# A fused attention and two mixture layers on one core: a gather issued earlier on POOL, two groups of transposes put ahead of a product, and the last row tile finished in two halves

## The chip, the cores and the metric

The kernel runs on one core of one Trainium2 chip. The metric is the device time of one execution in microseconds (us). The kernel before took 614.89 us, the median of 3 runs (614.12 to 617.11). An engine name stands for an instruction queue that runs in order: PE (TensorE, matrix products and transposes), ACT (ScalarE), DVE (VectorE), POOL (GpSimd, which also issues the indirect DMAs) and SP (SyncE, which issues the weight loads).

## The reference

Three stages follow each other, cut here to what is computed:

```
attn = softmax(q k^T / 8, masked) v          # B=2, H=8, S=576, D=64: 4 heads local, 4 heads strided
x    = attn as [1152 tokens, 512]
# first layer: one expert of 8 for each token
e    = argmax(x @ w_gate + modality_bias[modality_id])
x1   = gate * (relu(x @ w1[e]) @ w2[e])      # w1 512x1024, w2 1024x512 for each expert
# second layer: all 4 experts for each token, weighted
out  = sum over e of p[:, e] * (relu(x1 @ w1b[e]) @ w2b[e])
```

## The kernel before

**Order.** All instructions are issued in the order in which the Python code calls them; there is no planner. Work of different stages is interleaved by hand, with small hooks that are called at fixed places of a loop. Each engine runs its own instructions in that order, and waits where a semaphore says so.

**Precision.** Every fp32 operand of a large product is split into a rounded high part (ACT, a cast) and the remainder (DVE, a subtraction), and each product is three matmuls (high by high, high by low, low by high). `split` (lines 979 to 982) is this pair; its rows carry L981 for ACT and L982 for DVE.

**First layer.** Tokens are sorted by expert into 11 tiles of 128 rows (0 to 10). `moe1` (line 1141) runs a loop over k = 0 to 11. Round k does the first product of tile k (`mm1`, four blocks of weights, L1161), between them the transposes of the hidden rows of tile k-1 (`htr`, i = 0 and 1, L1168, four transposes each, followed by a split into hh and hl), and then the second product of tile k-1 (`mm2`, u = 0 to 3, six matmuls each, L1182 to L1184). After each mm2 it calls `mid(tile, u)`, and at the end of the round `after(tile)`. The result y goes from ACT to the DRAM buffer `ye` (L1228, L1230). In round 11 there is no first product: the products of unit 0 of the second layer are called through `before_last(W, n)` instead, which is `second_layer_start` (line 1494). Its table says how many products are called at n = 0 to 4.

**Weights of the first layer.** A block of 512 KB is loaded by SP into one of 8 staging places (L177), split by ACT and DVE into one of a ring of 10 pairs, and used by PE. The split of a block stands in the code up to 10 blocks ahead of its use (`W.ahead`), and as soon as DVE has done its part the place is free, and the load of the block that is next for this place may go. With a new expert every block is really loaded; with the same expert as the tile before, the load is skipped.

**From the first layer to the second.** The second layer wants the tokens in another grouping, in 9 chunks of 128 rows (j = 0 to 8). `x2_gather(j)` (L1240) is an indirect DMA on POOL's queue that reads rows of `ye` by the index tile `cidx` into a tile `g`; five `g` tiles are used in turn, together with the gathers of the first layer (L987). Chunk 2 reads only rows that tiles 0 to 4 have written (`lim`, line 1239). `x2_prep(j)` prepares a chunk in two steps: four transposes on PE (L1272), a copy back on ACT (L1274), four sums on POOL (L1278 to L1281) and splits (L1285 on ACT, L1286 on POOL); the second step splits the four sums. The table `PREP` (line 1473) says behind which (tile, u) each step stands: chunk 0 at (4, 2) and (5, 0), chunk 1 at (5, 2) and (6, 0), chunk 2 at (6, 2) and (7, 0), chunk 3 at (8, 2) and (9, 0). On POOL the row gathers of the first layer (L711, L987, called by `xprep` in the first-product part of a round) stand in the same queue.

**Second layer.** 32 units (16 for the first four chunks, 16 for the last five); `m2_unit` (line 1393) makes seven products (L1405 to L1407) of each, in a Strassen-like form, with sums of weight blocks on POOL (L1345 to L1348) and splits of weights in pieces (`PC`, L1324 on ACT, L1325 on DVE). `m2_mm2` (line 1547) makes the second products of the units into five accumulators, one for each row tile i (L1554, L1555, L1557). The products of row tiles 3 and 4 of the last three units are kept back in the list `late` and run last; after the last product of a row tile DVE multiplies and adds (L1567), and POOL scatters the rows to the output (`scatter`, L1577 and L1578).

Of the kernel before, what the change touches and what calls it, by code (L numbers as in the profile page):

```python
# [25 lines left out]
DM = H * D  # L26
# [100 lines left out]
def fused_kernel(  # L127
# [581 lines left out]
    def with_rows(y, idx, n=NTOK):  # L709

        nc.gpsimd.indirect_dma_start(  # L711
            out=y[:, DM:], out_offset=None, in_=xx[:n, :], in_offset=bass.IndirectOffsetOnAxis(ap=idx, axis=0)
        )
# [265 lines left out]
    def split(dst_h, dst_l, src):  # L979

        nc.scalar.copy(dst_h, src)  # L981
        nc.vector.tensor_tensor(dst_l, src, dst_h.bitcast(F32), op=ALU.subtract)  # L982
# [15 lines left out]
    def x_parts(g, pt=None):  # L998
        pt = pt or x_transposed(g)
        xh = xp.tile([P, 512], F32R, name="xh")  # L1000
        xl = xp.tile([P, 512], F32R, name="xl")
        split(xh, xl, pt)
        return xh, xl
# [137 lines left out]
    def moe1(mp, tiles, W, gs, pool, mid, after, before_last):  # L1141
        n = len(tiles)
        xs, hs, ys = {}, {}, {}

        def xprep(k):
            g = gs.pop(k)
            y = mp.tile([P, XW], F32, name="y", bufs=3)
            with_rows(y, idx16[:, tiles[k] : tiles[k] + 1])
            xs[k] = x_parts(g) if k > 1 else x01[k]
            ys[k] = y  # L1150
            if k + 2 < n:
                gs[k + 2] = m1_gather(tiles[k + 2], pool)

        def mm1(k, ph, kc):
            xh, xl = xs[k]
            key = "1", tiles[k], kc
            wh, wl = W.out.pop(key)
            s = slice(P * kc, P * (kc + 1))
            for xx, ww, first, last in ((xh, wh, kc == 0, False), (xh, wl, False, False), (xl, wh, False, kc == KC - 1)):
                for i in range(2):  # L1160
                    nc.tensor.matmul(ph[i], xx[:, s], ww[:, 512 * i : 512 * (i + 1)], start=first, stop=last)  # L1161
            W.release(key)

        def htr(k, i, ht):
            pt = pst.tile([P, 512], F32, name="ps_a")
            for c in range(4):
                s = slice(512 * i + P * c, 512 * i + P * (c + 1))
                nc.tensor.transpose(pt[:, P * c : P * (c + 1)], hs[k][:, s], ident)  # L1168
            hh = mp.tile([P, 512], F32R, name="hh")
            hl = mp.tile([P, 512], F32R, name="hl")  # L1170
            split(hh, hl, pt)
            ht.append((hh, hl))

        def mm2(k, ht, py, u):
            key = "2", tiles[k], u
            wh, wl = W.out.pop(key)
            for i in range(2):
                kc = 2 * u + i
                hh, hl = ht[kc // 4]
                s = slice(P * (kc % 4), P * (kc % 4 + 1))  # L1180
                f = slice(512 * i, 512 * (i + 1))
                nc.tensor.matmul(py, hh[:, s], wh[:, f], start=(kc == 0), stop=False)  # L1182
                nc.tensor.matmul(py, hh[:, s], wl[:, f], start=False, stop=False)  # L1183
                nc.tensor.matmul(py, hl[:, s], wh[:, f], start=False, stop=(kc == FC - 1))  # L1184
            W.release(key)

        xprep(0)
        xprep(1)
        for k in range(n + 1):
            ht = []  # L1190
            most = min(k, 1)
            if k == n:
                before_last(W, 0)
            if k < n:
                ph = [psb.tile([P, 512], F32, name="ps_b") for _ in range(2)]
                mm1(k, ph, 0)
            if k > 0:
                htr(k - 1, 0, ht)
            W.ahead(RING, most)
            if k == n:  # L1200
                before_last(W, 1)
            if k < n:
                mm1(k, ph, 1)
            if k > 0:
                htr(k - 1, 1, ht)
            W.ahead(RING, most)
            if k < n:
                mm1(k, ph, 2)
                if 0 < k < n - 1:
                    xprep(k + 1)  # L1210
                W.ahead(RING, most)
                mm1(k, ph, 3)
                h = mp.tile([P, FF], F32, name="h")
                for i in range(2):
                    nc.scalar.activation(h[:, 512 * i : 512 * (i + 1)], ph[i], AF.Relu)
                hs[k] = h
                W.ahead(RING, 1 + most)
            if k > 0:
                py = psb.tile([P, 512], F32, name="ps_b")
                for u in range(4):  # L1220
                    mm2(k - 1, ht, py, u)
                    if k == n and u < 3:
                        before_last(W, 2 + u)
                    mid(tiles[k - 1], u)
                    if u < 3:
                        W.ahead(RING, 1)
                y = ys.pop(k - 1)
                nc.scalar.activation(y[:, :DM], py, AF.Copy, scale=y[:, DM : DM + 1])  # L1228
                t = tiles[k - 1]
                nc.scalar.dma_start(out=ye[(t + 1) * P : (t + 2) * P, :], in_=y)  # L1230
                W.ahead(RING, 1)
                after(t)
# [4 lines left out]
    def x2_gather(j):  # L1237
        g = gp.tile([P, XW], F32, name="g")
        lim = min(NSX + 1, j + E1 + 1, 2 * j + 2) * P
        nc.gpsimd.indirect_dma_start(  # L1240
            out=g, out_offset=None, in_=ye[:lim, :], in_offset=bass.IndirectOffsetOnAxis(ap=cidx[:, j : j + 1], axis=0)
        )
        gx[j] = g
# [13 lines left out]
    CHT = (4, 5)  # L1257
# [207 lines left out]
    first, prep = {}, {}  # L1465

    def first_layer_start(t):
        for j in {3: (0,), 4: (1,), 5: (2,), 7: (3,)}.get(t, ()):
            x2_gather(j)
        prep_step(t, 4)  # L1470

# [3 lines left out]
    def prep_step(t, u):  # L1475
        j = PREP.get((t, u))
        if j is not None:
            next(prep.setdefault(j, x2_prep(j)), None)
        if (t, u) in ((NST - 2, 1), (NST - 2, 3)):
            PC.put((u + 1) // 2)  # L1480

    def first_layer_mid(t, u):
        if t >= 1 and u in (1, 3):
            next(place, None)
        prep_step(t, u)

    def first_tmp(k):
# [6 lines left out]
    def second_layer_start(W, n):  # L1494

        if n == 0:
            m2_bank.extend(psb.tile([P, 512], F32, name="ps_b") for _ in range(3))
            first["u"] = m2_unit(0, first_tmp)
        if n == 2:
            PC.put(2)  # L1500
        for _ in range((2, 0, 2, 2, 1)[n]):
            next(first["u"])


# [4 lines left out]
    W = Weights(m1b + m2b, raws, len(m1b))  # L1509
# [33 lines left out]
    for q in range(2):  # L1543
        t = xh2.rearrange("p q c t -> p (q c t)"), xl2.rearrange("p q c t -> p (q c t)")
        HT.append([x[:, NH * q : NH * (q + 1)].rearrange("p (f t h o) -> p f t h o", f=2, h=2, o=HP) for x in t])

    def m2_mm2(u, i, fh, cols=slice(0, DM)):

        c, e, fb = units2[u]
        hh, hl = (h[:, fh, i].rearrange("p h o -> p (h o)") for h in h_of(u))  # L1550
        wh, wl = (w[:, 512 * fh : 512 * (fh + 1)][:, cols] for w in WT["w", u])
        po = m2_acc[i][:, cols]
        part = (c, e, i) == (1, E2 - 1, CHT[1] - 1)
        nc.tensor.matmul(po, hh, wh, start=(fb == 0 and fh == 1), stop=False, skip_group_check=part)  # L1554
        nc.tensor.matmul(po, hh, wl, start=False, stop=False, skip_group_check=part)  # L1555
        last = fb == FC // 2 - 1 and fh == 0
        nc.tensor.matmul(po, hl, wh, start=False, stop=last, skip_group_check=part)  # L1557
        if last:
            j = CH0[c] + i
            if e == 0:  # L1560
                rows[j] = raws[KC + i // 2][:, DM * (i % 2) : DM * (i % 2 + 1)]
            pe = ext2[:, j, 1 + e : 2 + e]
            row = rows[j][:, cols]
            if e == 0:
                nc.vector.tensor_scalar(row, po, pe, None, op0=ALU.mult)
            else:
                nc.vector.scalar_tensor_tensor(row, po, pe, row, op0=ALU.mult, op1=ALU.add)  # L1567
            if e == E2 - 1 and cols.stop == DM:
                done.append(j)
                if c:  # L1570
                    scatter(done.pop(0))
# [32 lines left out]
    late = []  # L1604
    prep = {}
    for u in range(1, NU2):
# [10 lines left out]
        if u >= 4:  # L1617
            j, step = divmod(u - 4, 2)
# [3 lines left out]

    second(len(lag))
    late.sort(key=lambda x: (x[1], x[0], -x[2]))
    for x in late:
        if x[1] < CHT[1] - 1:
            m2_mm2(*x)
    for cols in (slice(0, DM // 2), slice(DM // 2, DM)):
        for x in late:
            if x[1] == CHT[1] - 1:  # L1630
                m2_mm2(*x, cols)

# [97 lines left out]
```

## Time and profile before

| what | value |
|---|---|
| median of 3 runs | 614.89 us |
| time of the profiled execution | 615.93 us |
| span of the profiled execution | 614.2 us |
| PE busy | 594.0 us, 97% of the span |
| DVE, ACT, POOL busy | 68%, 58%, 41% |
| mean granted TensorE clock | 0.989 of full speed |
| chain of work that ended last | PE 81%, DMA 2%, ACT 1%, DVE 1%, POOL 1% |

The span runs from the first to the last instruction; 1.7 us of the execution lie around it. An engine that is busy for a large share need not be the one that sets the end; the chain of waits and the idle time of PE tell that. A granted clock of 1.00 is 2.4 GHz, and 0.50 is 1.2 GHz.

### The profile page before, as it was taken

To read this page: it belongs to the slowest core of one execution; us is meant where nothing else is said; L and a number is where in the kernel's file an instruction comes from. 1 tells how busy PE (TensorE), PEld (TensorE's weight loads), DVE (VectorE), ACT (ScalarE), POOL (GpSimd) and SP (SyncE) were. 2 spreads that over 40 slices of the span, in tenths; PEclk is the share of its full clock that TensorE was granted. 3 is DMA by queue.
4 is the path that set the end of the run, shared out by engine and by line. 5 is a ranking of instruction groups with operands and counts; after the bars stand their busy time and mean duration, and the time that the engine had idled before them with its cause. 6 is when DMAs were issued, how large, how long until landed. Compare 5 with 4: busy or idle time off the path is not lost.

```text
span 614.2 us, 10457 instructions
## 1 busy us (share of the span) xinstructions
PE 594.0 (97%) x3649; PEld 498.9 (81%) x3649; DVE 420.1 (68%) x734; ACT 358.8 (58%) x703; POOL 250.4 (41%) x329
## 2 busy tenths in 40 slices
PE   8998999999989989999999999999999999999994
PEld 4565588887778879888989989999998889998883
DVE  5775789998969665676686686674575566557531
ACT  5763789989968755455565655544444444444410
POOL 6624341145943533555765856243322232222212
PEclk9999999999979989999999999999999999999998
DMA  8988225434786733442324232242222322222001
GB/s 255 320 232 295 91 53 171 136 117 129 229 291 228 277 118 114 146 148 77 129 70 138 69 107 101 74 149 86 103 69 69 109 97 70 68 69 70 1 9 77
DMA packets 34414, 79.27 MB, mean 129 GB/s; under 512 B 5936, under 2 KB 7866, under 8 KB 34229
## 3 DMA queue, kind: packets, MB, share of 16 engines
q1 hardware_dynamic: 28069, 65.64, 32.7%
q0 software_dynamic: 4272, 9.53, 5.1%
q10 hardware_dynamic: 2016, 3.39, 1.5%
q8 instruction: 30, 0.49, 0.3%
q14 instruction: 27, 0.22, 0.1%
HBM read 98.61 MB, written 9.28 MB: 176 GB/s over the span
## 4 chain that ended last, share of the span: by engine, by line
PE 81%; DMA 2%; ACT 1%; issue 1%; DVE 1%; POOL 1%; POOLq 0%; DVEq 0%
PE ps_b L1405 10%; PE ps_b L1406 10%; PE ps_b L1407 10%; PE ps_b L1161 9%; PE ps_b L1555 7%; PE ps_b L1554 7%; PE ps_b L1557 7%; PE ps_a L1554 4%; PE ps_a L1555 3%; PE ps_a L1557 3%; PE ps_b L1184 3%; PE ps_b L1182 3%; PE ps_b L1183 3%; PE ps_a L1168 1%; DMA g<-ye,cidx 1%
## 5 line engine op out<-in xcount | busy, mean ns | idle before, releaser
L1325 DVE TENSOR_TENSOR wl<-stage,wh 128x512 fp32r<-128x512 f32 (+1 forms) x160 | 125.2, 784 | 52.0 <-ACT wh L1324 51.1
L982 DVE TENSOR_TENSOR wl<-stage,wh 128x1024 fp32r<-128x1024 f32 x88 | 107.5, 1252 | 17.9 <-ACT wh L981 17.7
L1345 POOL TENSOR_TENSOR stage<-stage 128x256 f32<-128x256 f32 x32 | 24.1, 753 | 201.0 <-DVE wl L1325 201.0
L1324 ACT CAST wh<-stage 128x512 fp32r<-128x512 f32 (+1 forms) x160 | 102.8, 664 | 1.5 <-POOL stage L1348 1.5
L981 ACT CAST wh<-stage 128x1024 fp32r<-128x1024 f32 x88 | 89.7, 1056 | 5.2 <-ACT y L1228 2.3
L1417 DVE TENSOR_TENSOR m2t<-ps_b,stage 128x320 f32<-128x320 f32 (+1 forms) x93 | 42.2, 454 | 40.6 <-PE ps_b L1407 39.4
L1405 PE MATMUL ps_b<-xh,wh 128*128 128x256 f32 x224 | 64.0, 286 | 0.5 <-DVE xh L1417 0.5
L1406 PE MATMUL ps_b<-xl,wh 128*128 128x256 f32 x224 | 63.3, 283 | 0.0
L1407 PE MATMUL ps_b<-xh,wl 128*128 128x256 f32 x224 | 63.3, 282 | 0.0
L1405 PE MATMUL ps_b<-x,wh 128*128 128x320 f32 x160 | 49.6, 310 | 0.0
L1406 PE MATMUL ps_b<-x,wh 128*128 128x320 f32 x160 | 49.4, 309 | 0.0
L1407 PE MATMUL ps_b<-x,wl 128*128 128x320 f32 x160 | 49.4, 308 | 0.0
L1405 PEld LDWEIGHTS ps_b<-xh,wh 128*128 128x128 f32 x224 | 42.7, 191 | 5.9 <-DVE xh L1417 0.7
L1406 PEld LDWEIGHTS ps_b<-xl,wh 128*128 128x128 f32 x224 | 42.6, 190 | 4.4
L1420 ACT ACTIVATE hh2b<-m2t 128x256 fp32r<-128x256 f32 (+1 forms) x45 | 20.0, 444 | 43.7 <-DVE m2t L1417 41.8
L1420 ACT ACTIVATE hh2a<-m2t 128x256 fp32r<-128x256 f32 (+1 forms) x42 | 18.7, 445 | 43.9 <-DVE m2t L1417 43.9
L1407 PEld LDWEIGHTS ps_b<-xh,wl 128*128 128x128 f32 x224 | 42.7, 191 | 0.0
L1182 PE MATMUL ps_b<-wh,hh 128*128 128x512 f32 x88 | 35.9, 408 | 1.6 <-ACT hh L981 1.6
L1184 PE MATMUL ps_b<-wh,hl 128*128 128x512 f32 x88 | 35.7, 406 | 0.1
L1555 PE MATMUL ps_b<-wl,hh2a 128*128 128x512 f32 x90 | 35.5, 395 | 0.0
L1554 PE MATMUL ps_b<-wh,hh2a 128*128 128x512 f32 x90 | 35.5, 395 | 0.0
L1554 PE MATMUL ps_b<-wh,hh2b 128*128 128x512 f32 x90 | 35.5, 394 | 0.0
(286 smaller groups left out, 1538.1 us busy)
## 6 DMA issues: line engine op xcount, KB each, us to landing
stage<-in_w1a_dram SPq DMA_DIRECT2D x48, 512.0 KB
stage<-in_w2a_dram SPq DMA_DIRECT2D x48, 512.0 KB
stage<-in_w1b_dram SPq DMA_DIRECT2D x32, 512.0 KB
stage<-in_w2b_dram SPq DMA_DIRECT2D x32, 512.0 KB
ye<-y ACTq DMA_DIRECT2D x11, 260.0 KB
ye<-he SPq DMA_DIRECT2D x5, 260.0 KB
vl<-in_vlo_dram SPq DMA_DIRECT2D x2, 520.0 KB
xe<-rw POOLq DMA_DIRECT2D x7, 128.0 KB
```

The costliest lines, as they stand in the source:

```text
L981: nc.scalar.copy(dst_h, src)
L982: nc.vector.tensor_tensor(dst_l, src, dst_h.bitcast(F32), op=ALU.subtract)
L1161: nc.tensor.matmul(ph[i], xx[:, s], ww[:, 512 * i : 512 * (i + 1)], start=first, stop=last)
L1182: nc.tensor.matmul(py, hh[:, s], wh[:, f], start=(kc == 0), stop=False)
L1324: return (lambda: nc.scalar.copy(h[:, s], src[:, s])), (lambda: nc.vector.tensor_tensor(l[:, s], src[:, s], h[:, s].bitcast(F32), op=ALU.s ...
L1325: lambda: nc.vector.tensor_tensor(l[:, s], src[:, s], h[:, s].bitcast(F32), op=ALU.subtract)
L1405: nc.tensor.matmul(ph, wh[:, kc], xh, start=first and kc == 0, stop=False, skip_group_check=True)
L1406: nc.tensor.matmul(ph, wh[:, kc], xl, start=False, stop=False, skip_group_check=True)
L1407: nc.tensor.matmul(ph, wl[:, kc], xh, start=False, stop=kc == 1, skip_group_check=True)
L1554: nc.tensor.matmul(po, hh, wh, start=(fb == 0 and fh == 1), stop=False, skip_group_check=part)
L1555: nc.tensor.matmul(po, hh, wl, start=False, stop=False, skip_group_check=part)
L1557: nc.tensor.matmul(po, hl, wh, start=False, stop=last, skip_group_check=part)
```

## The change

Three places are touched. The gather of chunk 2 is called behind mm2(5, 0), no longer at the end of the round of tile 5. In round 11 both groups of transposes of tile 10 are called between the first and the second product of unit 0, no longer behind both. At the end, the first half of the columns of row tile 4 is called ahead of row tile 3, and the second half behind it.

```diff
             if k == n:
                 before_last(W, 0)
+                for i in range(2):
+                    htr(k - 1, i, ht)
+                before_last(W, 1)
             if k < n:
                 ph = [psb.tile([P, 512], F32, name="ps_b") for _ in range(2)]
                 mm1(k, ph, 0)
-            if k > 0:
+            if 0 < k < n:
                 htr(k - 1, 0, ht)
             W.ahead(RING, most)
-            if k == n:
-                before_last(W, 1)
             if k < n:
                 mm1(k, ph, 1)
-            if k > 0:
+            if 0 < k < n:
                 htr(k - 1, 1, ht)
...
     def first_layer_start(t):
-        for j in {3: (0,), 4: (1,), 5: (2,), 7: (3,)}.get(t, ()):
+        for j in {3: (0,), 4: (1,), 7: (3,)}.get(t, ()):
             x2_gather(j)
...
     def first_layer_mid(t, u):
         if t >= 1 and u in (1, 3):
             next(place, None)
+        if (t, u) == (5, 0):
+            x2_gather(2)
         prep_step(t, u)
...
-        for _ in range((2, 0, 2, 2, 1)[n]):
+        for _ in range((1, 1, 2, 2, 1)[n]):
             next(first["u"])
...
+    last = [x for x in late if x[1] == CHT[1] - 1]
+    for x in last:
+        m2_mm2(*x, slice(0, DM // 2))
     for x in late:
-        if x[1] < CHT[1] - 1:
+        if x not in last:
             m2_mm2(*x)
-    for cols in (slice(0, DM // 2), slice(DM // 2, DM)):
-        for x in late:
-            if x[1] == CHT[1] - 1:
-                m2_mm2(*x, cols)
+    for x in last:
+        m2_mm2(*x, slice(DM // 2, DM))
```

## Rows read from the trace of the kernel before

**Rows 1.** The page's part 2: granted TensorE clock in 40 slices, tenths.
```profile
PEclk9999999999979989999999999999999999999998
```
**Rows 2.** Waits of PE from 80 to 222 us: total, times, longest.
```profile
PE ps_b L1272 <- DMA g<-ye,cidx: 2.7, 1, 2.7
PE ps_b L1182 <- ACT hh L981: 1.6, 1, 1.6
```
**Rows 3.** The chain of waits in order of time: start, length, what.
```profile
141.91 0.44 PE ps_b L1272 x4
...
163.92 6.81 DMA g<-ye,cidx
170.78 1.11 PE ps_b L1272 x4
...
174.45 2.56 PE ps_b L1161 x6
...
177.46 1.40 PE ps_b L1161 x6
```
**Rows 4.** Stretches: length, busy PE, PEld, DVE, ACT, POOL; clock, DMA share, GB/s.
```profile
148.80:162.00 13.20, 13.19 (x65) 10.67 (x66) 12.52 (x12) 12.54 (x20) 11.31 (x11) 1.00 0.70 218
...
160.00:162.00 2.00, 2.00 (x12) 1.49 (x11) 2.00 (x3) 2.00 (x4) 2.00 (x4) 1.00 0.81 228
...
174.00:176.00 2.00, 2.00 (x7) 1.52 (x6) 1.47 (x1) 1.25 (x3) 2.00 (x4) 0.50 1.01 387
```
**Rows 5.** Timeline of POOL and DVE, 148 to 170 us: start, length, instruction, idle before.
```profile
151.18 1.26 POOL L987 DMA_INDIRECT g<-xe,idx  x1 [0.30 <-PE ps_b L1161]
153.56 2.08 POOL L1286 TENSOR_TENSOR xl<-ye,xh 128x512 fp32r<-128x512 f32 x1 [1.12 <-ACT xh L1285]
...
161.49 2.28 POOL L1286 TENSOR_TENSOR xl<-g,xh 128x128 fp32r<-128x128 f32 x3
163.92 1.79 POOL L1240 DMA_INDIRECT g<-ye,cidx  x1 [0.15 <-PE ps_b L1161]
...
152.14 7.12 DVE L982 TENSOR_TENSOR wl<-stage,wh 128x1024 fp32r<-128x1024 f32 x5
```
**Rows 6.** Timeline of ACT, 145 to 207 us.
```profile
145.26 0.33 ACTq L1230 DMA_DIRECT2D ye<-y  x1
...
165.99 0.66 ACT L1285 CAST xh<-ye 128x512 fp32r<-128x512 f32 x1
...
171.93 0.58 ACT L1274 COPY g<-ps_b 128x512 f32<-128x512 f32 x1 [3.40 <-PE ps_b L1272]
...
206.67 1.05 ACT L981 CAST wh<-stage 128x1024 fp32r<-128x1024 f32 x1 [0.36 <-DMA stage<-in_w2a_dram]
```
**Rows 7.** Timeline of PE around the first unit, 214 to 222 us.
```profile
214.21 1.04 PE L1168 MATMUL ps_a<-mk,h 128*128 128x128 f32 x8
216.87 0.50 PE L1182 MATMUL ps_b<-wh,hh 128*128 128x512 f32 x1 [1.62 <-ACT hh L981]
...
221.75 0.39 PE L1182 MATMUL ps_b<-wh,hh 128*128 128x512 f32 x1
```
**Rows 8.** Timeline of ACT and DVE over the same stretch.
```profile
215.41 0.62 ACT L1324 CAST wh<-stage 128x512 fp32r<-128x512 f32 x1 [0.96 <-POOL stage L1348]
...
216.25 1.05 ACT L981 CAST hh<-ps_a 128x512 fp32r<-128x512 f32 x2
...
216.06 0.69 DVE L1325 TENSOR_TENSOR wl<-stage,wh 128x512 fp32r<-128x512 f32 x1 [0.70 <-ACT wh L1324]
...
217.00 1.28 DVE L982 TENSOR_TENSOR hl<-ps_a,hh 128x512 fp32r<-128x512 f32 x2
```
**Rows 9.** Timeline of PE and POOL at the end.
```profile
603.54 0.38 PE L1554 MATMUL ps_a<-wh,hh2b 128*128 128x256 f32 x1 [0.58 <-DVE stage L1567]
...
602.40 0.96 POOL L1578 DMA_INDIRECT out_dram<-stage,oid  x1 [1.38 <-DVE stage L1567]
...
607.25 0.98 POOL L1578 DMA_INDIRECT out_dram<-stage,oid  x1 [3.69 <-issue]
```

## The prediction

> **What bounds the kernel now.** I read the clock row first. It shows full speed but for the start, the end and two dips, in slices 12 and 15, that is about 169 to 184 and 215 to 230 us [rows 1]. Then the waits of PE: between 80 and 222 us it stands idle twice only, 2.7 us for the gathered rows of a chunk and 1.6 us for an hh of ACT [rows 2]. The chain of waits passes through the first: gather at 163.92, then 6.81 us until its rows are there, then four transposes at 170.78 [rows 3]. So PE, busy for 97% of the span, sets the end from 74 us on, and a gain is a PE stall that goes, provided no other engine is late in its place. Each stall costs more than its idle time: behind it the clock is at 0.50, 1.2 GHz [rows 4], and matmuls take nearly twice as long [rows 3].
>
> **Part 1, the gather of chunk 2.** The transposes of chunk 2 stand behind mm2(6, 2), which ends at 168.06 (170.78 less 2.72 of idle). The gather goes at 163.92 only because POOL works off chunk 1's sums and splits first, until 163.77 (161.49 + 2.28) [rows 5]. In the new order its place on POOL is behind the row gather that starts at 151.18 and ends at 152.44, ahead of the split of 153.56, which waits 1.12 us for ACT anyway [rows 5]. The gather needs three things: `cidx`, used by two gathers already; rows of tiles 0 to 4, the last of which ACT sent off at 145.26 [rows 6], 7 us earlier, and whose y tile the row gather of tile 7, ahead in POOL's queue, has to wait for as well (three y tiles in turn); and a free g tile, the one of tile 7's rows, transposed in that round's first-product part, ahead of mm2(5, 0). So it goes at about 152.7, lands by 159.6 even with the same 6.81 us, and is 8 us early.
>
> What PE gets back, from rows 3: 2.72 idle; transposes 1.11 instead of 0.44 = 0.67; six mm2 from 171.89 to 174.45, 2.56 instead of 1.40 (a first-product row of six matmuls of the same shape) = 1.16; the next six first-product matmuls 2.56 instead of 1.40 = 1.16. Sum 5.71.
>
> What the moved gather costs: it holds POOL for 1.2 to 1.8 us (the row gather took 1.26, the gather itself 1.79) [rows 5], of which 1.1 us were idle, so chunk 1's sums end up to 0.7 later; ACT asks for them at 165.99 and they ended before 161.49, 4.5 us of cover [rows 5, 6]. The two row gathers for tiles 8 and 10, behind the gather in the old order, go about 1 to 2 us earlier. No new wait is added to PE's queue.
>
> Does something else become late? ACT and DVE are busy 12.54 and 12.52 of 13.20 us in a round that also prepares a chunk, with PE never idle [rows 4]; in the stall ACT stood idle for 3.40 us [rows 6], which it will not have. By the lengths of its instructions ACT then runs behind the shifted PE by about 2.2 us at the first split of the next round and has made it up at the end of it; the second product needs the first hh 5 us after its transposes, so this is covered. The loads: SP's triggers come 3.5 to 5 us earlier. A block is 0.524 MB; at 387 GB/s, which the queue moved when it was full [rows 4], that is 1.35 us, and sixteen blocks from 161 on, with the gathers and results between, take about 27 us, to 188.8; the last of them is split at 198 now and at 192.4 then, 3.6 us of cover. I take 5.6 of the 5.71. The bounds: 5.7 if nothing is late; 0 if the feed is late by the whole stall.
>
> A rule of the Trainium skill speaks against this part (page "SBUF — State Buffer", section "SBUF: two separate sides"): the port pair that VectorE and GpSimd share is locked for whole instructions, and descriptors of a POOL DMA can't be written while VectorE holds it. Here DVE does run five two-input subtractions without a gap, from 152.14 to 159.26 [rows 5], just where the gather now stands. If POOL were shut out for all of them, the gather would still land by 167, but chunk 1's sums would end at about 168.6, ACT would wait 2.6 us at 165.99, and the hidden rows of the next round would come about 0.5 us late: the sum would be 8.7 instead of the 9.2 below. The row gather of 151.18 and the splits from 153.56 ran among such subtractions in 1.26 and 2.08 us, so the lock is passed on between instructions, and I add nothing.
>
> **Part 2, the transposes ahead of the second product of unit 0.** The stall: ACT's cast of a weight piece waits until 215.41 for POOL's sums, and both hh stand behind it, at 216.25 [rows 8]; PE starts mm2(10, 0) at 216.87 after 1.62 idle, and half clock follows [rows 7]. From 214.21, where the transposes start, to 221.75, unit 1 of mm2(10), PE takes 7.54 us for eight transposes (0.88), six 128x512 matmuls (1.40) and twelve of half the width (1.40), 3.68 at full clock. In the new order the transposes stand 0.70 earlier (six half-width matmuls), and the hh go ahead of the cast. hh0 is done at about 215.0, hl0 (0.64 each) at 215.65, PE asks for it at 215.57: 0.1 to 0.2 of wait. DVE then has hl1, the add of the second product and the piece's subtraction (0.69) [rows 8], to about 217.25; the third matmul of the next product asks at 216.85: 0.4. The next piece again: 0.4. So about 1.0 of small waits instead of 3.86 of idle and half clock: 2.9. The bounds: 3.9 with no wait left; 0.5 if the small waits bring the clock down as before.
>
> **Part 3, the last row tile.** Now PE waits 0.58 us between the two halves of row tile 4, for DVE, which reads the first [rows 9]; with row tile 3's 4.1 us of matmuls between them this cover is complete. PE's matmuls are the same, so the last one, DVE's multiply and the scatter come 0.7 earlier (idle plus the restart of a first matmul of 0.38). What moves the other way is the scatter of row tile 3: from 602.40 to about 604.4, off POOL (0.96 and a 0.19 cast) at 605.6, where the last is due at 607.25 - 0.7 = 606.5 [rows 9]. Gain 0.7; bounds 0 (the last scatter queues) and 0.75.
>
> **Sum.** 5.6 + 2.9 + 0.7 = 9.2. Span 614.2 - 9.2 = 605.0; the profiled execution took 615.93 (1.73 around the span), so 606.7; the median of the runs shown lies 1.04 below that execution: 614.89 - 9.2 = 605.7, the forecast. Behind 222 us the longest wait of PE is the 0.58 of rows 9, so what is won is kept.
>
> **Rivals.**
> (a) The clock falls at unit 0 all the same. For: idle time in pieces within 3 us, where a single stall of 1.62 did it. Against: it is 1.0 us in three pieces with matmuls between them. Part 2 gives 0.5: 614.89 - 6.8 = 608.1.
> (b) The feed takes back half of part 1: ACT or DVE, at 95% in such a round, stay behind PE, and a stall of 1 to 3 us shows in rounds 8 to 10. For: the 12.5 of 13.2 us. Against: PE was never idle in that round [rows 4], and the round of tile 7 to follow, without a first step of a chunk, is lighter. 614.89 - 9.2 + 2.8 = 608.5.
> (c) The gather is held back on POOL, so that it doesn't go before about 160 (an index, slot or store wait that I misread). For: a wait that was over before 163.77 is invisible. POOL's sums go with it, so part 1 gives nothing: 614.89 - 3.6 = 611.3.
> (d) Slower: the loads. They moved at 228 GB/s with a share of 0.81 at 160 to 162 [rows 4]. If that is all they can do, a block takes 2.3 us, sixteen end at 198.5 and the four of tile 10's second product at 207.8, where ACT takes the last at 206.67 now [rows 6] and would want it at 201.1. Then tile 10 ends 1.1 later than now, with one more fall of the clock (3.0) and parts 1 and 2 gone: 614.89 + 4.1 - 0.7 = 618.3. It decides from the point at which a block takes over 1.6 us. Against: 387 GB/s, and ACT waits for loads by 0.36 only [rows 6].
>
> **How the numbers follow.** Forecast 0.65, (a) 0.13, (b) 0.10, (c) 0.07, (d) 0.05. A measurement of this kernel tells some 0.5%, 3 us, from no change: faster is below 611.8. Forecast, (a) and (b) are, and most of (c), whose 611.3 lies at the bound: 0.92 faster, 0.04 the same, 0.04 slower. The range runs from all bounds taken, 5.7 + 3.9 + 0.75 = 10.4 with 0.5 of scatter, 604.0, up past (a) and (b) with some scatter, 609.2; it leaves out (c) and (d) and a little on the low side.
>
> **What would show it.** Right: L1240's third row near 152.7 on POOL; L1272 near 168.1 without idle time and 0.44 long; no slice with a clock below 0.9 between 92 and 600 us; hh0 ahead of the cast of the weight piece on ACT; waits of PE between 208 and 214 us (the old 214 to 220) of 0.5 and less; the last two halves without a wait on L1567. Wrong: idle time of PE on hh, xh or wl in rounds 8 to 10, an ACT wait for staging blocks of over 1 us, a clock of 0.5 behind the first unit, a gather that lands after 168.

## The result and the profile after

The changed kernel took 608.79 us, the median of 6 runs (607.90 to 610.05), against 614.76 us for the kernel before in 6 runs (613.55 to 617.11): a ratio of 0.990, 95% interval 0.988 to 0.992. It is faster, inside the range of the prediction, but by 6.0 us and not by the 9.2 that were worked out. The profiled execution took 608.43 us with a span of 606.6, 7.6 below the span of before.

The clock row of the page, 40 slices in tenths of full speed, has lost both dips of [rows 1]:

```profile
PEclk9999999999999999999999999999999999999998
```

The waits of PE from 80 to 620 us (total, times, longest) no longer hold either row of [rows 2]. There is a new one at their head, of 1.4 us:

```profile
PE ps_b L1406 <- ACT stage L1439: 1.4, 1, 1.4
PE ps_b L1406 <- DVE xh L1418: 0.5, 1, 0.5
PE ps_b L1408 <- DVE wl L1326: 0.2, 1, 0.2
PE ps_b L1406 <- DVE xl L1426: 0.2, 1, 0.2
```

**The gather.** Timeline of POOL, 148 to 170 us (start, length, instruction, idle before; most lines are one or a few numbers higher than in the kernel before). It answers to [rows 5]:

```profile
150.68 1.27 POOL L987 DMA_INDIRECT g<-xe,idx  x1 [0.30 <-PE ps_b L1161]
152.25 1.43 POOL L1241 DMA_INDIRECT g<-ye,cidx  x1 [0.30 <-issue]
153.70 1.45 POOL L1287 TENSOR_TENSOR xl<-ye,xh 128x512 fp32r<-128x512 f32 x1
...
161.05 2.29 POOL L1287 TENSOR_TENSOR xl<-g,xh 128x128 fp32r<-128x128 f32 x3
```

The gather of chunk 2 goes at 152.25, right behind the row gather, 11.7 us earlier, and chunk 1's splits are not later for it: 161.05, where they started at 161.49. DVE was subtracting without a gap at the same time:

```profile
151.65 4.58 DVE L982 TENSOR_TENSOR wl<-stage,wh 128x1024 fp32r<-128x1024 f32 x3
```

So the gather was not shut out for the run of subtractions, the price that the prediction weighed and did not take: it took 1.43 us inside these 4.58, less than the 1.79 of [rows 5], more than the 0.98 of the same gather in the trace of part 3 alone, and nothing waited for it. The Trainium skill (page "SBUF — State Buffer", section "SBUF: two separate sides") says that two SBUF inputs of VectorE lock the shared port pair only against a GpSimd operation that reads SBUF, so its rule may not bear on this gather at all. On PE the transposes of chunk 2 follow mm2(6, 2) with no idle time, and everything behind them is at full clock, where [rows 3] had 2.56 us for six matmuls:

```profile
167.28 0.40 PE L1184 MATMUL ps_b<-wh,hl 128*128 128x512 f32 x1
167.52 0.60 PE L1273 MATMUL ps_b<-mk,g 128*128 128x128 f32 x4
...
170.75 0.49 PE L1168 MATMUL ps_a<-mk,h 128*128 128x128 f32 x3
```

**The transposes of tile 10.** Timeline of ACT, 207 to 214 us, in place of the first rows of [rows 8]; both hh now stand ahead of the cast that waits for POOL's sums:

```profile
208.52 1.08 ACT L981 CAST hh<-ps_a 128x512 fp32r<-128x512 f32 x2
210.17 0.62 ACT L1325 CAST wh<-stage 128x512 fp32r<-128x512 f32 x1 [0.56 <-POOL stage L1349]
```

PE over the same stretch, for [rows 7]: the only noted idle time is 0.22, and mm2(10, 1) starts at 213.09 instead of 221.75.

```profile
207.67 1.04 PE L1168 MATMUL ps_a<-mk,h 128*128 128x128 f32 x8
...
211.57 0.39 PE L1408 MATMUL ps_b<-xh,wl 128*128 128x256 f32 x1 [0.22 <-DVE wl L1326]
...
213.09 0.40 PE L1182 MATMUL ps_b<-wh,hh 128*128 128x512 f32 x1
```

**The new stall.** PE in unit 1 of the second layer:

```profile
227.37 0.39 PE L1406 MATMUL ps_b<-xh,wh 128*128 128x256 f32 x1 [1.44 <-ACT stage L1439]
```

ACT's timeline shows what it waits for: not the copy of L1439 itself, but the write ahead of it, the first into `hh2b`, which waits for the last store of y into `ye`:

```profile
221.47 0.33 ACTq L1231 DMA_DIRECT2D ye<-y  x1
...
226.64 0.42 ACT L1421 ACTIVATE hh2b<-m2t 128x256 fp32r<-128x256 f32 x1 [3.91 <-DMA ye<-y]
226.96 0.35 ACT L1439 COPY stage<-ps_b 128x256 f32<-128x256 f32 x1
```

`hh2b` belongs to the buffers that are laid out for the second layer, and lies where the y tiles of the first layer were. In the profiled execution of the kernel before the same wait was there too, with 1.90 us of idle ACT time and none on PE (ACT's timeline):

```profile
229.72 0.33 ACTq L1230 DMA_DIRECT2D ye<-y  x1
...
232.87 0.42 ACT L1420 ACTIVATE hh2b<-m2t 128x256 fp32r<-128x256 f32 x1 [1.90 <-DMA ye<-y]
```

ACT goes on 5.17 us after the store's issue (226.64 - 221.47) where it was 3.15 (232.87 - 229.72). What differs is what SP sent off ahead of the store: two weight blocks of 512 KB. Here are SP's timelines, before and then after:

```profile
227.22 0.34 SPq L177 DMA_DIRECT2D stage<-in_w1b_dram  x1
227.60 0.44 SPq L177 DMA_DIRECT2D stage<-in_w2b_dram  x1
```
```profile
220.15 0.34 SPq L177 DMA_DIRECT2D stage<-in_w1b_dram  x1
220.53 0.43 SPq L177 DMA_DIRECT2D stage<-in_w2b_dram  x1
```

Before, the blocks were 2.1 to 2.5 us ahead of the store, after 0.9 to 1.3. Two further executions of the kernel before, below, show that the 1.90 is not what this kernel always has there.

**The end.** Timeline of PE and POOL. The last matmul starts at 598.17 (605.67 before), and the last scatter 7.51 us earlier than in [rows 9], with 0.70 us of idle POOL ahead of it:

```profile
598.17 0.28 PE L1560 MATMUL ps_a<-wh,xl 128*128 128x256 f32 x1
```
```profile
597.88 0.96 POOL L1581 DMA_INDIRECT out_dram<-stage,oid  x1 [3.53 <-DVE stage L1570]
...
599.74 0.98 POOL L1581 DMA_INDIRECT out_dram<-stage,oid  x1 [0.70 <-POOL oid L1580]
```

### The profile page after: what moved, and what is told of

Same layout as the page of the kernel before. It is cut to its first block, busy times and chain, and to the rows that moved or that the text cites. A ratio compares the mean times of both kernels' runs of the same rounds, so it can differ in the third digit from the quotient of the medians.

```text
span 606.6 us, 10457 instructions
## 1 busy us (share of the span) xinstructions
PE 589.6 (97%) x3649; PEld 494.9 (82%) x3649; DVE 420.9 (69%) x734; ACT 358.5 (59%) x703; POOL 254.0 (42%) x329
## 4 chain that ended last, share of the span: by engine, by line
PE 68%; ACT 6%; DVE 6%; issue 3%; DMA 2%; POOL 1%; ACTq 0%; POOLq 0%; DVEq 0%
PE ps_b L1406 10%; PE ps_b L1407 9%; PE ps_b L1408 9%; PE ps_b L1558 7%; PE ps_b L1557 7%; PE ps_b L1560 7%; DVE wl L982 4%; PE ps_b L1161 4%; PE ps_a L1557 4%; PE ps_a L1558 4%; PE ps_a L1560 4%; ACT wh L981 3%; DMA stage<-in_w2a_dram 1%; PE ps_b L1184 1%; PE ps_b L1183 1%
## 5 line engine op out<-in xcount | busy, mean ns | idle before, releaser
L982 DVE TENSOR_TENSOR wl<-stage,wh 128x1024 fp32r<-128x1024 f32 x88 | 108.9, 1271 | 11.7 <-ACT wh L981 11.4
L1418 DVE TENSOR_TENSOR m2t<-ps_b,stage 128x320 f32<-128x320 f32 (+1 forms) x93 | 42.1, 453 | 39.9 <-PE ps_b L1408 38.8
L1558 PE MATMUL ps_b<-wl,hh2b 128*128 128x512 f32 x90 | 35.5, 394 | 0.0
L1560 PE MATMUL ps_b<-wh,hl2b 128*128 128x512 f32 x90 | 35.4, 394 | 0.0
```

Source lines behind the costliest of these rows:

```text
L1418: nc.vector.tensor_tensor(t, a, b, op=ALU.add)
```

## The experiments

The question was where the missing 3 us of the forecast are. Theory: the three parts work as described, but (1) the store of y now holds up unit 1, and (2) the two falls of the clock in [rows 1] are no fixed part of the kernel before. Rival: one part doesn't give what its place in the trace suggests, because the feed or the clock takes it back elsewhere. Ratios are against the kernel before on the same chip.

To compare executions I use three lengths that PE's timeline gives. **A**: from the last matmul of mm2(6, 2) to the first transposes of round 8 (before: 167.66 to 176.81). **B**: from the first product of unit 0 to mm2(10, 1) (212.79 to 221.75). **C**: from there to the last matmul (605.67). All in us, one profiled execution each:

| execution | A | B | C | span |
|---|---|---|---|---|
| before, first | 9.15 | 8.96 | 383.92 | 614.2 |
| before, second | 8.05 | 7.52 | 384.63 | 611.8 |
| before, third | 7.06 | 7.37 | 384.45 | 610.6 |
| part 1 alone | 3.46 | 9.26 | 383.95 | 609.2 |
| part 2 alone | 8.13 | 6.12 | 385.20 | 613.6 |
| part 3 alone | 4.52 | 8.24 | 383.88 | 609.0 |
| whole change, first | 3.47 | 6.12 | 385.08 | 606.6 |
| whole change, second | 3.46 | 6.12 | 384.60 | 608.4 |
| whole change, third | 3.45 | 6.11 | 384.57 | 605.9 |
| whole, other layout | 3.45 | 6.53 | 383.12 | 604.9 |
| whole, store first | 3.47 | 6.41 | 383.46 | 605.2 |

**Part 1 alone.** The two hunks that move the call `x2_gather(2)`.

> Only the gather of chunk 2 is moved. Theory: the three parts act at three places and add up, so this one alone gives what the two profiles show for it, 5.3 to 5.5 us: median about 609.4, clock dip in slice 12 gone, the one in slice 15 still there with 1.6 us of idle time, no stall in unit 1. Rival (the feed takes part of it back when part 2 doesn't help): 2 to 4 us, with PE idle on hh or wl in rounds 8 to 10.

Measured: 611.33 us in 12 runs, ratio 0.997 (0.995 to 0.999). That is 2.1 us, not the 5.3 to 5.5 that were expected from one pair of profiles. A is as short as in the whole change. The wait for hh is still there, now 2.18 us where the three executions of the kernel before have 1.56 to 1.74, with half clock behind it: PE comes to this wait earlier, and part of what was won is lost there. The one longer wait for hh, 2.44 in part 3 alone, belongs to the next shortest A.

**Part 2 alone.** The hunks of `moe1` and the table of `second_layer_start`.

> Only the two groups of transposes are moved. Theory: this part wins 2.8 us at unit 0 and itself makes the new stall of 1.4 us in unit 1 (ACT waits for the last y store to land), with which 1.9 to 2.0 us are given back: 0.9 us in all, median about 613.9. Rival (the new stall comes from the first part, by its earlier loads): no stall in unit 1 here and 2.8 us, median about 612.0.

Measured: 611.98 us, ratio 0.998 (0.995 to 1.000), so a gain is likely but not clear of the noise. B is as short as in the whole change; the gather's stall is there with 2.88 us; and unit 1 has its new stall, 0.69 us. Part 1 alone doesn't show it. Part 3 alone, whose edit acts only at the end, shows 0.23 at this place (its lines are one number lower):

```profile
229.74 0.39 PE L1405 MATMUL ps_b<-xh,wh 128*128 128x256 f32 x1 [0.23 <-ACT stage L1438]
```

So the stall is not made by part 2 alone: it can come without it, and part 2 makes it larger.

**Part 3 alone.** The hunk of `late`.

> Only the row tile at the end is reordered. Theory: 0.7 to 0.8 us, median about 614.0, no wait of PE on L1567 at the end. Rival (the last scatter queues behind that of row tile 3): 0, with the last scatter issued more than 0.8 us behind the last multiply and add of DVE.

Measured: 613.07 us, ratio 1.001 (0.998 to 1.004): the 0.7 is below what this can show. By their medians the three parts alone give 2.1, 1.5 and 0.4 us, 4.0 together. The profile was worth more. Both stalls of [rows 2] are still in this kernel, and in this execution neither brought the clock down (PE's timeline; then the two stretches with their length, the busy time of PE, PEld, DVE, ACT and POOL, the granted clock, which is 1.00 in both, the DMA share and GB/s):

```profile
169.08 0.66 PE L1272 MATMUL ps_b<-mk,g 128*128 128x128 f32 x4 [0.82 <-DMA g<-ye,cidx]
...
213.32 0.50 PE L1182 MATMUL ps_b<-wh,hh 128*128 128x512 f32 x1 [2.44 <-ACT hh L981]
```
```profile
170.00:174.00 4.00, 4.00 (x21) 3.23 (x21) 2.41 (x3) 3.52 (x7) 3.43 (x5) 1.00 0.92 294
214.00:220.00 6.00, 5.35 (x33) 4.67 (x33) 4.37 (x7) 2.70 (x6) 3.48 (x4) 1.00 0.53 175
```

The stall of 2.44 us is longer than the 1.62 of [rows 7], and there is no fall behind it. The gather's stall of 0.82 is the shortest of its kind here.

**The kernel before twice more**, unchanged, one profiled execution each.

> The kernel before once more, one profiled execution, for the size of the two stalls and for the clock behind them. If the falls are a fixed part of the kernel before, as the prediction took them: L1273's counterpart L1272 waits 2.7 us for g and hh 1.6 us, and a clock of 0.5 follows both. If they come and go from execution to execution: the waits lie anywhere in 0.8 to 2.9 and 1.6 to 2.5 us, and one or both stretches show a clock of 1.00.

> As the run ahead of it: a second profiled execution of the kernel before, to see whether its stalls and falls of the clock are those of the first.

Second execution, waits of PE (total, times, longest) and the two stretches, 170 to 174 and 214 to 220 us:

```profile
PE ps_b L1272 <- DMA g<-ye,cidx: 2.8, 1, 2.8
PE ps_b L1182 <- ACT hh L981: 1.7, 1, 1.7
```
```profile
170.00:174.00 4.00, 3.57 (x12) 2.90 (x13) 0.58 (x1) 2.58 (x6) 2.82 (x7) 0.63 1.02 361
214.00:220.00 6.00, 4.46 (x24) 3.65 (x25) 4.45 (x8) 4.78 (x10) 1.55 (x2) 1.00 0.24 72
```

Third execution, with waits of 1.8 and 1.6 us, the same two stretches:

```profile
170.00:174.00 4.00, 4.00 (x14) 3.27 (x13) 1.00 (x1) 2.92 (x6) 3.38 (x7) 0.60 1.00 363
214.00:220.00 6.00, 5.47 (x30) 4.40 (x30) 4.99 (x8) 3.75 (x8) 2.50 (x3) 1.00 0.41 136
```

Both fall behind the gather's stall, neither behind the wait for hh, which is about as long as in the first (1.74 and 1.56, against 1.62). The fall behind the gather is shorter too: A is 8.05 with a stall of 2.82, where 2.72 gave 9.15.

These two also show the wait for the last store at its usual length. Their loads go 1.2 to 1.6 us ahead of the store, and ACT is idle for 2.99 and 2.82 us, not 1.90. ACT's timeline of the second:

```profile
226.72 0.33 ACTq L1230 DMA_DIRECT2D ye<-y  x1
...
230.98 0.42 ACT L1420 ACTIVATE hh2b<-m2t 128x256 fp32r<-128x256 f32 x1 [2.99 <-DMA ye<-y]
```

C is 0.7 and 0.5 longer than in the first. So the kernel before itself loses time in unit 1 in these two, in which the clock does not fall at unit 0.

**The whole change twice more.** The second execution was timed in 12 runs.

> The whole change once more, on the chip of the three that follow. Theory (the two falls of the clock in the profile of before, some 5 us, come in a part of the executions only, so that the median holds only a part of them): 4.5 to 6 us faster than before, no execution of before with a clock of 0.997 slower than 613, and among such executions alone the gain is about 4. Rival (the falls are there in nearly every execution of before, and the missing 3 us are the new stall alone): 6 us, and clocks of before at 0.989 to 0.991.

> The whole change once more, one profiled execution beside the two of the kernel before. Expected: no idle time at the gather of chunk 2, no clock under 0.9 from 166 to 222 us, a stall of unit 1 of 0.8 to 1.5 us with an ACT idle of 3.4 to 4 us for the last y store; a span of 606 to 609, 2 to 3 us below an execution of the kernel before that has no fall of the clock, and 6 to 8 below one that has two.

Measured: 610.22 us against 614.33 for the kernel before, ratio 0.993 (0.990 to 0.996), and one execution of 607.75 on another chip, where the kernel before took 614.41. So the 12 runs gain 4.1 us, less than the 6.0 of the first result and than the 4.5 to 6 expected, and 610.22 lies above the range of the prediction. A and B are the same to 0.02 us in all three, while the kernel before spreads over 2 us in each. Unit 1's stall is 0.9 in both (ACT idle for 3.40 ahead of `hh2b`). In the second the clock dips at 56 to 61 us, a stretch that the change doesn't touch; it does so in the trace of part 2 alone as well.

**Filling the stalls in the kernel before.** Unused transposes keep PE at work in front of both waits; the waits themselves stay.

```diff
+            for _ in range(14 if k == n else 0):
+                nc.tensor.transpose(m2_bank[2][:, :P], ident, ident)
...
+        for _ in range(22 if j == 2 else 0):
+            nc.tensor.transpose(pt[:, :P], ident, ident)
```

> The kernel before, with PE given 22 needless 128x128 transposes ahead of those of chunk 2, and 14 ahead of mm2(10, 0), into banks that are written afresh behind them: the two stalls are filled (2.4 and 1.5 us), nothing is moved, and the wanted work starts when it did. It prices the clock apart from the idle time. Theory (the falls are the stalls' doing, but come only in a part of the executions): clock at 1.00 behind both places, median 1 to 2 us below before, and no execution under 0.993. Rival (each stall brings a fall nearly always): 4 to 5 us below before. Rival (the falls have nothing to do with the stalls): no gain, or up to 0.5 us lost, and a fall in the trace all the same.

Measured: 613.90 us, ratio 1.000 (0.997 to 1.003). No fall in its trace at either place, and no gain that the runs show: the interval leaves some 2 us either way. The rival of 4 to 5 us falls; the 1 to 2 us expected is not shown. A is 5.87 and B 8.11, where the change has 3.47 and 6.12, and PE still waits 0.8 for hh. The filling takes its full 2.56 us also where the stall would have been 0.8. Keeping the clock up alone doesn't give what the change gives.

**Loads held back.** Unit 3's two loads called later in the code, in place of what SP issues ahead of the store.

> The whole change, but the two weight loads that SP issues 0.9 to 1.3 us ahead of the last y store are held back to the next release of a place, some 8 us. Theory (the store lands late because it stands behind these 1 MB in the DMA engines): the store lands in about 3 us, ACT's idle time ahead of L1421 falls from 3.9 to below 2 us, PE's stall of 1.4 us in unit 1 is 0.3 or less, 1.4 to 1.9 us less than the whole change unless unit 3 is then short of weights, which would show as a PE wait on wh or wl between 235 and 250 us. Rival (the store needs 5 us by itself): stall and time as in the whole change.

Measured: 609.69 us, ratio 0.993 (0.990 to 0.996), but it tests nothing: SP had nothing else in its queue, and issued both loads at 226.38 and 226.77, still ahead of the store at 227.70. ACT was idle for 3.36 us and PE for 0.8, as without the edit. In its profiled execution (614.15) the clock is at half from 34 to 41 us, again a stretch that no edit touches.

**Another place in memory.** Three of the tiles that unit 0 uses are laid out ahead of `hh2b`, so that this lies elsewhere.

```diff
+    x1 = [m2p.tile([P, 2 * HX], F32R, name=f"x1_{i}") for i in range(3)]
     HT.append([m2p.tile([P, 2, max(CHT), 2, HP], F32R, name=n) for n in ("hh2b", "hl2b")])
...
-    spare += [m2p.tile([P, 2 * HX], F32R, name=f"x1_{i}") for i in range(10)]
+    spare += x1 + [m2p.tile([P, 2 * HX], F32R, name=f"x1_{i}") for i in range(3, 10)]
```

> The whole change, and three tiles that are used late are placed ahead of hh2b, so that hh2b no longer lies where the y tiles were; every instruction and its order stay the same. Theory (ACT's first write to hh2b waits until the last y store has been read from that memory): the stall of 1.4 us in unit 1 is gone, 1.7 to 2.0 us less than the whole change, median about 606.9. Rival (ACT is late there by the pace of the weight pieces and of POOL's sums, the store only lands in the same moment): same time as the whole change, 608.8, ACT still idle 3 us and more ahead of L1421.

Measured: 609.00 us in 10 runs, ratio 0.995 (0.992 to 0.998). In the trace ACT no longer waits for the store, 1.66 us after its issue, and unit 1's stall is gone:

```profile
221.59 0.33 ACTq L1231 DMA_DIRECT2D ye<-y  x1
...
223.25 0.42 ACT L1421 ACTIVATE hh2b<-m2t 128x256 fp32r<-128x256 f32 x1 [0.40 <-DVE m2t L1418]
```

C is 383.12 instead of 384.57 to 385.08. B has become 0.4 longer, so B and C together are 1.0 to 1.6 shorter. That is too little for the timed runs to show; the median of 606.9 that was expected did not come.

**The store first.** In the whole change, unit 3's two loads are issued from ACT's queue, right behind the last store of y.

```diff
-            W.load()
+            if u != 1:
+                W.load()
...
+    W.load(nc.scalar)
```

> The whole change, with the two weight blocks of unit 3, which SP issues at 220.15 and 220.53, ahead of the last y store of 221.47, issued instead from ACT's own queue right behind that store. Theory (the store is late because two blocks of 512 KB are less than 1.4 us ahead of it): the store lands about 3.1 us after its issue, as where the loads were 2.1 to 2.5 us ahead; ACT's idle time before its first write of hh2b falls from 3.91 to 2.0 or less, the stall of PE in unit 1 from 0.8 to 1.4 us to 0.3 or less; 0.8 to 1.9 us less than the whole change by itself. Rival (the store takes 4.4 to 5.2 us by itself, or other traffic of that stretch holds it up): ACT idle for 3.4 or more, PE's stall stays at 0.8 to 1.4, time as with the whole change. A third outcome: the later loads make unit 3's splits late, then a new wait on a staging block shows behind 228 us and the time is not less.

Measured: 607.51 us in 4 runs, ratio 0.990 (0.984 to 0.995). ACT's timeline:

```profile
221.55 0.33 ACTq L1231 DMA_DIRECT2D ye<-y  x1
221.90 0.46 ACTq L177 DMA_DIRECT2D stage<-in_w1b_dram  x1
222.39 0.48 ACTq L177 DMA_DIRECT2D stage<-in_w2b_dram  x1
...
223.84 0.42 ACT L1423 ACTIVATE hh2b<-m2t 128x256 fp32r<-128x256 f32 x1
```

The write into `hh2b` starts 2.29 us after the store's issue and waits for nothing, so the store had landed by then, against 5.17 with the same loads ahead of it. The rival, that a store takes 4.4 to 5.2 us by itself, falls. PE has no wait in unit 1, C is 383.46, B and C together are 0.8 below the better two of the whole change.

**The layout and another table.** The other layout, and one product of unit 1 moved behind: `(1, 1, 2, 1, 2)` in `second_layer_start`.

> The whole change with the three tiles ahead of hh2b, and in the table of the last round (1, 1, 2, 1, 2) for (1, 1, 2, 2, 1), so that six matmuls of the last tile stand between the two products of unit 0 that use one bank. Theory: the wait of 0.5 us on L1418 there goes too, and PE has no wait over 0.3 us between 75 us and the end: about 0.5 less than with the three tiles alone, 2.2 less than the whole change. Rival (the fourth product of that round then meets another wait, on hl2a or on a piece of unit 1): 0.

Measured: 607.47 us in 6 runs, ratio 0.989 (0.984 to 0.994), with a span of 605.4. The waits of unit 1 and on L1418 are gone, and PE's longest wait is 0.89 at the gather of chunk 1. By its median it is 2.75 below the whole change on the same chip (610.22). The intervals of the two ratios overlap, but of the 12 runs of the whole change only two (607.64, 608.41) are as low as the highest of these six (609.04), so it is likely the faster one. Neither of the other two variants is shown by its time to beat the change.

## Why the prediction held, and which of its steps did not

**The bound and the mechanisms held.** PE set the end; removing its two long waits moved everything behind them. Part 1: the gather was forecast near 152.7 and went at 152.25, the transposes near 168.1 without a wait and came at 167.52. Part 2: B lost 2.84 in the profiled pair, 2.9 forecast, with the order on ACT and the small waits that were named. Part 3: the wait between the halves is gone, and no scatter queues.

**Step that failed: "what is won is kept".** It rested on PE's waits behind 222 us, and a wait that PE doesn't see isn't in that view. ACT's 1.90 us for the last store was covered by PE's own lateness in the execution that was read. In the whole change the wait is 3.40 to 3.91, and 0.9 to 1.4 of it comes through as idle PE time. In the first pair, C is 385.08 against 383.92: 1.16 longer, although part 3 had taken 0.82 out of it (the last matmul came 6.68 us earlier just before part 3's place, 7.50 at the end). The give-back is 8.66 - 6.68 = 1.98, where 8.66 is what mm2(10, 1) was earlier (221.75 to 213.09). All of it arises within unit 1: 1.44 of idle time, the rest in the slower starts of two products behind it.

ACT's idle time ahead of `hh2b` goes with nearly all of the spread of C (0.82 added to C where part 3 is in; us):

| execution | ACT idle | C without part 3 |
|---|---|---|
| whole, other layout | 0.40, not for the store | 383.94 |
| whole, store first | none | 384.28 |
| part 1 alone | 1.86 | 383.95 |
| before, first | 1.90 | 383.92 |
| before, third | 2.82 | 384.45 |
| before, second | 2.99 | 384.63 |
| part 3 alone | 3.08 | 384.70 |
| part 2 alone | 3.17 | 385.20 |
| whole, second and third | 3.40 | 385.42, 385.39 |
| whole, first | 3.91 | 385.90 |

The 1.86 and 1.90 belong to the two executions in which the clock fell at unit 0, with the loads 2.1 to 2.5 us ahead of the store. So the prediction read the wait in an execution that happened to hide it. Against the other two executions of the kernel before the change gives back 0.8 to 1.5, not 1.98; some 0.5 to 0.7 of what the fall at unit 0 cost was not there to be won, as the executions of the kernel before without that fall lose as much in unit 1. Two repairs that go at the wait from different sides, the store's place in the queue and the place of `hh2b`, both take the stall out.

**Terms that were mis-sized: the falls of the clock.** The sum held 2.99 us of half clock in part 1 (0.67 + 1.16 + 1.16) and 2.24 in part 2 (3.86 less 1.62). Both were true of the profiled execution and were taken as true of the kernel. Of five profiled executions that still had the gather's stall, four had a fall behind it; of five with the wait for hh, two had. The gather's stall itself was 0.82 (without a fall), 1.81, 2.72, 2.82 and 2.88 us long. What part 1 takes out is therefore A less 3.47: 1.05 to 5.68. For part 2, B less 6.12, it is 1.25 to 3.14. The second execution of before against the third of the change is a plain case: 4.60 + 1.41 + 0.06 = 6.1, with spans 5.9 apart, the gain of the medians. The forecast 5.6 + 2.9 + 0.7 describes an execution with both falls, no give-back in C and the upper end of part 1's stall.

The other timed runs fit this. Of 70 runs of the kernel before, 25 had a mean granted clock of 0.995 or more, with a median of 612.03 us, and 21 had 0.991 or less, with a median of 616.10. Of 19 of the change, 12 had 0.995 or more (608.79) and one 0.991 or less (613.61). On the chip that ran both in number, the gain between runs of 0.995 or more is 2.5 (612.03 to 609.57). So part of the gain goes with executions of low clock becoming rare. A mean doesn't tell where the clock fell, and it also falls at 34 to 61 us in some executions, so it is not shown that the two stalls account for all of this.

**Rivals.** (a) The clock didn't fall at unit 0 with the change in any trace. (b) and (d), the feed: DMA moved 377 GB/s from 172 to 184 us with PE busy for 11.94 of 12.00 us, so neither came:

```profile
172.00:184.00 12.00, 11.94 (x59) 9.48 (x58) 11.50 (x12) 11.36 (x16) 9.51 (x9) 1.00 1.01 377
```

(c) The gather was not held. The case that came, a give-back on ACT behind 222 us, was not among them; the range held the first result because its upper end, 609.2, reached past (a) and (b), which was luck, and the median of the 12 later runs lies outside it.

**What stays open.** Why the gather's rows took 5.4 us in one execution (issue to transposes, 163.71 to 169.08, the issuing instruction 0.98 long) and 6.9 in another (163.92 to 170.78, 1.79 long), and what decides whether the clock falls behind a wait of 1.6 to 2.4 us. Why the gain was 6.0 us in one set of runs and 4.1 in another is open too, beyond the spread that the falls bring.

## What to carry to other kernels

Price a stall by its idle time in several executions, and put a fall of the clock behind it into the range, not into the sum, until a second trace shows it too. Before writing that a gain is kept, list the waits of the other engines behind the place, with the slack that PE's lateness gave them: the one that is due next is there, with its length, and not among PE's waits. Where a buffer of the next stage lies on one whose store is still under way, what is issued just ahead of that store on any queue belongs to the wait.

## What the runs showed that was not expected

How long a store of one y tile is awaited goes with how closely two loads of 512 KB were sent off ahead of it: 3.1 us behind its issue where they were 2.1 to 2.5 us ahead (two executions), 4.1 to 4.3 where they were 1.2 to 1.6 ahead (four), 4.4 to 5.2 where they were 0.9 to 1.3 ahead (five), and no more than 2.29 where they came behind it, though the loads ahead of it stand in SP's queue and the store in ACT's. The Trainium skill says as much (page "DMA: Bandwidth & Descriptors", section "Issuing engines are not separate DMA queues"): DMAs of different engines end up on the same 16 DMA engines, and the trace agrees.

A wait of PE of 1.62 us was followed by a clock of 0.50 (1.2 GHz) and one of 2.44 us at the same place of the code by 1.00.
